# Second-layer groups of fifteen products in two blocks of two steps each

## The chip, the cores and the metric

The kernel runs on one core of a Trainium2 chip. The core has a matrix engine (TensorE, "PE" in the profile; "PEld" is its loading of weights), a vector engine (VectorE, "DVE"), a scalar engine that evaluates functions (ScalarE, "ACT"), a general engine (GpSimd, "POOL") and queues of transfers (started by SyncE, "SP"). Matrix products are accumulated in PSUM, a small memory of eight banks, from which only DVE and ACT read. The metric is the time of one execution on the device, in microseconds (us); less is better.

## The reference

The input x has 2048 rows of 512 numbers. After a layer norm, two branches are computed and multiplied. Branch A is attention with 32 heads of width 16, all on one common set of keys and values; branch B is a layer of 1792 units with the Mish function, and a second layer back to 512.

```python
xn = _layernorm(x)
q  = (xn @ wq)            # 32 heads of 16
k, v = xn @ wk, xn @ wv   # one key and one value head for all
p  = softmax(q k^T / 4)   # 32 x 2048 x 2048
s  = (p v) @ wo
h  = xn @ w1 + b1
g  = silu((h * tanh(softplus(h))) @ w2)
out = x + s * g
```

## The kernel before

**The work of attention.** The 2048 rows are cut into four chunks of 512 (`C`), and the 32 heads into eight sets of four; that makes 32 units of attention, and each unit goes over the 16 blocks of 128 keys. One such block of keys is a *step*; there are 512 steps (`NS`). In a step PE makes four score products `e` (64 rows of the array, 512 columns; L886), ACT takes the exponential of each from PSUM into a tile of `pts` (L893), and two steps later PE multiplies the four tiles with the values (`pv`, L971, on 128 rows, in four column strips of 32; the profile counts eight instructions for one step). The softmax needs the maximum over the keys first: for the units ahead, PE makes four products `m` in each step (L915), and DVE takes the maximum of each from PSUM (L919, one `reduce_max` of 128x512). `e` and `m` have three PSUM banks each (`ps_e`, `ps_m`, L124 and L125), the sum of `pv` and the sum `xps` of the other matrix products one bank each. `pts` has 14 tiles (`NPT`).

**The other matrix products.** They come in *groups* that sum into `xps`: the projection of the queries (`q_group`), the first layer (`m1_group`), the second layer (`m2_groups`) and the output projection (`wo_groups`). Numbers are split in a high and a low part, and three products replace one: a group over four blocks of rows is 12 products. The second layer is cut in thirds of 5, 5 and 4 blocks (`THIRDS`), so that its first two thirds are groups of 15 products and the last is groups of 12; there are 32 groups of 15 (four chunks, two thirds, four tiles of 128 rows). At the end of a group, one engine fetches the sum from `xps`: ACT for the first third (`y<-xps`, L718) and for the first layer (`hb`, L655), DVE for the second and last third (an addition, L722).

**How they share the array.** A product of a group is made in two halves of 64 rows (`half`, L111). In each step one half is used: the halves of the group's products run on 64 rows of the array, while `e` and `m` run on the other 64 rows at the same time. `waves` (L524) writes this interleaving. A group is cut in chunks of at most 8 products (`XMAX`, `chunk_size`); a chunk takes two steps, one for each half. So 12 products are two chunks of 6, and 15 are a chunk of 8 and one of 7; both take four steps. At the end of each step stand ACT's other jobs (`act_jobs`) and the `pv` of two steps before. So the array changes between 64 rows and 128 rows twice in each step.

**What sets the order.** The order of all engines is written by this program itself. The loop at L1312 goes through the steps; `begin` (L472) takes the next group whose operands are thought to be there. What is "there" is found from a count of POOL's time (`busy`, `charge`, `pool_at`) and of SP's (`sp_at`), which are turned into steps with one length for all steps (`STEP_US`, 2.95 us). Weights come by DMA (`load`), and POOL splits them in two parts (`split`); the ring `ws` holds two of the first layer's blocks, the ring `wb` five of the second layer's. Instructions of one engine run in the order in which they are written, so a product whose operand is late holds up all of PE behind it. An instruction that would overwrite a PSUM bank waits for the reader of the bank's last content; a new tile of a pool takes the buffer whose last reader stands earliest in the program.

**Ahead of and behind the steps.** Before step 0 a lead of about 90 us (`LEAD` in the code counts steps at the end) makes the layer norm, the keys and values and the first maxima; PE fills its idle time there with products of groups (`fill`), or with products that nothing uses (`warm`). In the last 22 steps no maxima are left to make, and the rest of the groups runs on all 128 rows between `e` and `pv`.

```python
n = m_sides(1 - h, k // 2) if inm else 0        # m beside the k halves; 4 - n on the halves' own rows
...
waves(h, em, inm)
act_jobs(1 + (len(jobs) > 2))
due(s + 0.5)
if s >= 2:
    pv(s - 2)
```

Of the kernel before, what the change touches and what calls it, by code (L numbers as in the profile page):

```python
# [14 lines left out]
F32 = mybir.dt.float32  # L15
# [5 lines left out]
P = 128  # L21
# [29 lines left out]
TMAX = 2.0 ** 14  # L51
EMAX = 2.0 ** 60
# [33 lines left out]
class Group:  # L86
    def __init__(self, mms, post, items=(), after=(), pre=None, start=None, wo=None, alloc=None):
        self.mms, self.post, self.items, self.after, self.pre = mms, post, items, after, pre
        self.start, self.wo, self.alloc = start, wo, alloc
        self.done = None  # L90
        self.m1 = None
        self.dve = False
        self.late = len(self.items)
        for i in items:
            i.users += 1

    def slack(self, k):
        return 2 if k >= self.late else 0


class Mm:
# [18 lines left out]
def block_kernel(ctx: ExitStack, tc: tile.TileContext, x, wq, wk, wv, wo, w1, b1, w2, out):  # L120
# [13 lines left out]
    lead = {}  # L134
    busy = [-10.0 ** 7]

    def charge(us):
        busy[0] = max(busy[0], step[0] * STEP_US + (0 if lead else 1.5)) + us

    sp_t = [-10.0 ** 7]  # L140

    def sp_at(us):

        sp_t[0] = max(sp_t[0], step[0] * STEP_US) + us
        return (sp_t[0] + 2.6) / STEP_US - 1

    def pool_at(margin):
        return max(math.ceil(2 * (busy[0] / STEP_US + margin)) / 2, step[0])

    def hi_pool(o, i):  # L150
        charge(0.7)
# [231 lines left out]

    def arrived(tag):
        k, n = todo[tag]
        return k < n and items[tag][k].step + 1 <= (step[0] if lead else max(step[0], busy[0] / STEP_US) + 0.3)

    def home(tag, k):
        if tag == "wx":
# [5 lines left out]
    def split(tag):  # L395
        k = todo[tag][0]
        it = items[tag][k]
        w = home(tag, k)
        if not lead:
            busy[0] = max(busy[0], (it.step + 1) * STEP_US)  # L400
# [29 lines left out]
    def load(tag):  # L430
        its = items[tag]
        k, n = todo[tag]
        if tag == "wx" and m1_done.get((NC - 2, NFT - 1)) is None:
            return
        if n == len(its) or n >= RING[tag] and its[n - RING[tag]].users or lead and tag == "wb" and n and now[0] < kept_at.get(3, 1e9):
            return
# [20 lines left out]
            load(tag)  # L457

    held = [None]
    evacs = [0]  # L460
    cur = {"g": None, "ps": None, "n": 0, "chunk": [], "relay": None}

# [8 lines left out]

    def begin():  # L472
        prepare()
        if qqueue and is_ready(qqueue[0]):
# [49 lines left out]
    def waves(h, em, new):  # L524
# [10 lines left out]
        k = len(mms)  # L535
        ms = em(k)
        a = deque(ms[1 - h])
        b = deque(ms[h])
# [38 lines left out]
    def mm12(lhs, rhs, n):  # L577
        res = []
        tot = 3 * n
        for j in range(n):  # L580
            for a, b in TERMS:
                res.append(Mm(pe, lambda j=j, a=a: lhs(j, a), lambda j=j, b=b: rhs(j, b), len(res), tot))
        return res

    qt_of = {}
    xt_done = {}
# [118 lines left out]
    def m2_groups(c, third, its, m1s):  # L705
        lo, hi = THIRDS[third]

        def ready():
            done = m1_done.get((c, hi - 1))
            return None if done is None else done - 2  # L710

        def mk(tt):
            def post(ps):
# [24 lines left out]
                def s3():  # L738
# [5 lines left out]
                later(0.5, lambda: job(s1, t_free))  # L744

            g = Group(mm12(lambda j, a: act_of[c, lo + j][:, a, P * tt:P * (tt + 1)],
                           lambda j, b: its[j].tile[:, b], hi - lo), post, its, [ready])
            g.dve = third > 0
            g.late = 3 if hi - lo == 5 else 2
            return g  # L750
        return [mk(tt) for tt in range(4)]

# [122 lines left out]
    def e_one(s, i):  # L875

        v, r = divmod(s, 16)
        if s < NS - LEAD:
            a, k, p = 1 - s % 2, r - r % 2 + i // 2, i % 2
        else:  # L880
            a, k, p = i % 2, r, i // 2
        q = qt_of[v]
        o = 64 * a
        ps, tag = (ps_m, "m") if NS - LEAD <= s and i in ((1, 3) if s < NS - 8 else (3,)) else (ps_e, "e")
        e = ps.tile([P, C], F32, tag=tag, name=f"e{s}_{i}")
        pe.matmul(e, ks[o:o + 64, P * k:P * (k + 1)], q[o:o + 64, p], start=True, stop=True)  # L886
        z = None
        if i > 1 and s % 4 == 1 and PAIRS[0] < s < PAIRS[1]:
            pt = sb.tile([P, C], F32, tag=("qh", "ql")[i - 2], name=f"pt{s}_{i}", bufs=1)
        else:  # L890
            z = pt_free.popleft()
            pt = pts[:, z]
        r = act.activation(pt, e, AF.Exp, scale=0.25)  # L893
        if z in pt_last:
            tc.declare_no_dep(r.ins, pt_last[z].ins, reason="the value products that read the tile lie between")
        if z is not None:
            pt_last[z] = r
        pt_of[16 * v + k, p, a] = pt, z
        return r

    m_next = [0, 0]

    def m_one(a):
# [5 lines left out]
        kb, j = divmod(n, 8)  # L909
        p, t = divmod(j, 4)  # L910
        o = 64 * a
        ps, tag = (ps_e, "e") if lead and 15 in xp_of and a else (ps_m, "m")
        m = ps.tile([P, C], F32, tag=tag, name=f"m{v}_{a}_{n}")
        o = slice(o, o + (HALF if v < len(qts) else 48))
        pe.matmul(m, q[o, p, P * t:P * (t + 1)], ks[o, C * kb:C * (kb + 1)], start=True, stop=True)  # L915
# [310 lines left out]
    while True:  # L1226
# [46 lines left out]
                task("SP", 2.6, move, [r1])  # L1273
        elif k == "X":
            fresh = cur["g"] is None
            if cur["g"] is not None or not waiting and begun[0] < 1 + (s - 18) / X_US and begin():
# [6 lines left out]
                T["PE"] = s + 0.25  # L1283
                kind[0] = "X"
        elif k == "J":
            tag = next((g for g in ("wq", "ws", "wb") if arrived(g) and busy[0] + E0 < s + 0.5), None)
            n = ran[0]
            if tag:
                split(tag)
# [19 lines left out]
    lead.clear()  # L1309

    rowq = deque()
    for s in range(NS + 2000):  # L1312
        inm = s < NS - LEAD
        if inm or cur["chunk"]:
            assert s < NS
            due(s)
# [53 lines left out]
            if s >= NS:  # L1370
                fill(16)
        step[0] = s
        if vdone[0] < 8 * NC and min(m_next) >= m_need(vdone[0]):
            r = c_rows(vdone[0])
            rowq.extend([r[0], r[1], lambda r=r: (r[2](), r[3]())])
            vdone[0] += 1
        if rowq and not evacs[0]:
            rowq.popleft()()
        evacs[0] = 0
        pump()  # L1380
        if s > NS + 1 and not queue and cur["g"] is None and not timed and not jobs:
            break
# [12 lines left out]
```

## Time and profile before

| | |
|---|---|
| median of 3 runs | 1600.07 us (1599.21 to 1601.7) |
| the profiled execution | 1599.22 us |
| its span, first to last instruction | 1597.4 us |
| PE busy | 1579.5 us, 99% of the span |
| DVE busy | 1345.5 us, 84% |
| ACT busy | 1292.7 us, 81% |
| POOL busy | 620.1 us, 39% |
| mean granted clock of TensorE | 0.999 |

The span is one execution as the hardware profiler saw it; the time has 1.8 us around it. The page shows the busy time of each engine, the span in 40 slices, the chain of work that ended last, and groups of instructions with their mean duration and with the idle time of their engine before them. Two matrix products that run on different rows of the array at the same time both have their own row; so the sum of the durations exceeds the busy time, and what a step costs is read from the starts of the rows. The timeline has one row for instructions of the same kind that follow each other, with their count.

### The profile page before, as it was taken

To read this page: it belongs to the slowest core of one execution; us is meant where nothing else is said; L and a number is where in the kernel's file an instruction comes from. 1 tells how busy PE (TensorE), PEld (TensorE's weight loads), DVE (VectorE), ACT (ScalarE), POOL (GpSimd) and SP (SyncE) were. 2 spreads that over 40 slices of the span, in tenths; PEclk is the share of its full clock that TensorE was granted. 3 is DMA by queue.
4 is the path that set the end of the run, shared out by engine and by line. 5 is a ranking of instruction groups with operands and counts; after the bars stand their busy time and mean duration, and the time that the engine had idled before them with its cause. 6 is when DMAs were issued, how large, how long until landed. Compare 5 with 4: busy or idle time off the path is not lost.

```text
span 1597.4 us, 31240 instructions
## 1 busy us (share of the span) xinstructions
PE 1579.5 (99%) x11660; PEld 843.1 (53%) x11660; DVE 1345.5 (84%) x2299; ACT 1292.7 (81%) x2490; POOL 620.1 (39%) x628
## 2 busy tenths in 40 slices
PE   8999999999999999999999999999999999999998
PEld 5455555555555555555555555555555555555543
DVE  8988888888988988888898988888889998888811
ACT  5478788789898778978889787887898878789785
POOL 3876158155365102422525222252252414226311
PEclk9999999999999999999999999999999999999999
DMA  5332133142141315112113221230332212031020
GB/s 163 146 116 84 35 109 121 27 150 77 45 135 53 103 27 176 57 35 86 50 56 96 76 92 45 96 97 16 123 97 84 73 57 96 16 107 45 17 78 27
DMA packets 72775, 127.30 MB, mean 80 GB/s; under 512 B 21488, under 2 KB 34288, under 8 KB 72112
## 3 DMA queue, kind: packets, MB, share of 16 engines
q1 hardware_dynamic: 72624, 125.30, 25.0%
q8 instruction: 93, 1.52, 0.4%
q14 instruction: 58, 0.48, 0.1%
HBM read 76.36 MB, written 27.26 MB: 65 GB/s over the span
## 4 chain that ended last, share of the span: by engine, by line
PE 93%; DVE 2%; POOL 2%; ACT 2%; DMA 1%; issue 0%; SPq 0%; DVEq 0%; POOLq 0%; ACTq 0%
PE xps L113 46%; PE pv L971 31%; PE m L915 8%; PE e L886 5%; PE xps L109 2%; PE wop L109 1%; DVE mb L919 1%; PE warm L1204 1%; PE kp L296 0%; ACT pts L893 0%; DMA w<-wbs 0%; ACT pts L199 0%; POOL hb L157 0%; DVE st L221 0%; DMA pts<-in_dram 0%
## 5 line engine op out<-in xcount | busy, mean ns | idle before, releaser
L919 DVE TENSOR_REDUCE mb<-m 128x1 f32<-128x512 f32 x2048 | 1271.9, 682 | 177.6 <-PE m L915 151.9
L893 ACT ACTIVATE pts<-e 128x512 f32<-128x512 f32 x2042 | 1065.5, 605 | 245.7 <-PE e L886 237.2
L915 PE MATMUL m<-ks,qt 48*128 48x512 f32 (+1 forms) x2048 | 841.3, 421 | 0.6 <-DVE mb L919 0.2
L886 PE MATMUL e<-qt,ks 64*128 64x512 f32 x2048 | 735.7, 402 | 1.4 <-ACT pt L893 1.4
L971 PE MATMUL pv<-pts,vaug 128*32 128x512 f32 x4084 | 543.8, 604 | 0.0
L915 PEld LDWEIGHTS m<-ks,qt 48*128 48x128 f32 (+1 forms) x2048 | 371.7, 185 | 54.0 <-DVE mb L919 21.2
L886 PEld LDWEIGHTS e<-qt,ks 64*128 64x128 f32 x2048 | 372.9, 186 | 23.0 <-ACT pts L893 12.1
L113 PE MATMUL xps<-xt,ws 64*128 64x512 f32 x1248 | 346.1, 410 | 2.2 <-POOL ws L157 1.2
L113 PE MATMUL xps<-wbs,act 64*128 64x512 f32 x1248 | 337.4, 407 | 0.0
L113 PEld LDWEIGHTS xps<-xt,ws 64*128 64x128 f32 x1248 | 215.1, 185 | 207.4 <-ACT pts L893 135.8
L113 PEld LDWEIGHTS xps<-wbs,act 64*128 64x128 f32 x1248 | 217.5, 185 | 179.4 <-ACT pts L893 112.5
L971 PEld LDWEIGHTS pv<-pts,vaug 128*32 128x32 f32 x4084 | 81.3, 108 | 143.7 <-issue 134.7
L167 POOL TENSOR_SCALAR t<-t 128x512 f32<-128x512 f32 x56 | 34.4, 615 | 310.7 <-ACT t L661 310.4
L157 POOL TENSOR_TENSOR hb<-hb,t 128x512 f32<-128x512 f32 x56 | 72.3, 1290 | 75.7 <-ACT t L674 54.1
L113 PE MATMUL xps<-xt,wq 64*128 64x512 f32 x336 | 93.0, 409 | 0.0
L113 PEld LDWEIGHTS xps<-xt,wq 64*128 64x128 f32 x336 | 58.0, 185 | 55.4 <-ACT pts L893 35.2
L157 POOL TENSOR_TENSOR oc<-oc,sc 128x512 f32<-128x512 f32 (+1 forms) x16 | 20.6, 1285 | 160.7 <-ACT sc L999 121.3
L113 PE MATMUL xps<-wbs,ot_all 64*128 64x512 f32 x288 | 79.3, 408 | 0.0
L113 PEld LDWEIGHTS xps<-wbs,ot_all 64*128 64x128 f32 x288 | 49.5, 184 | 47.0 <-ACT pts L893 29.3
L157 POOL TENSOR_TENSOR hb<-hb,u 128x512 f32<-128x512 f32 x56 | 72.3, 1291 | 4.4
L157 POOL TENSOR_TENSOR act<-hb,act 128x512 fp32r<-128x512 f32 x56 | 72.1, 1287 | 4.7
L157 POOL TENSOR_TENSOR u<-u,t 128x512 f32<-128x512 f32 x56 | 71.9, 1284 | 4.7
(120 smaller groups left out, 814.6 us busy)
## 6 DMA issues: line engine op xcount, KB each, us to landing
ws<-w SPq DMA_DIRECT2D x38, 512.0 KB
wbs<-w SPq DMA_DIRECT2D x36, 512.0 KB
qt<-qh SPq DMA_DIRECT2D x256, 32.0 KB
w<-ws SPq DMA_DIRECT2D x14, 512.0 KB
w<-wbs SPq DMA_DIRECT2D x14, 512.0 KB
wq<-wq SPq DMA_DIRECT2D x13, 512.0 KB
wbs<-wo SPq DMA_DIRECT2D x12, 512.0 KB
rawwb<-in_dram SPq DMA_DIRECT2D x20, 256.0 KB
```

Source lines behind the costliest of these rows:

```text
L109: self.pe.matmul(ps, self.lhs(), self.rhs(), start=(self.k == 0), stop=(self.k == self.tot - 1))
L113: i = self.pe.matmul(ps, self.lhs()[o], self.rhs()[o], start=(self.k == 0 and self.halves == 0), stop=(self.k == self.tot - 1 and self.hal ...
L157: eng.tensor_tensor(out=o, in0=a, in1=b, op=op)
L167: pool.tensor_scalar(o, o, lim, 0.0, op0=ALU.min, op1=ALU.max)
L886: pe.matmul(e, ks[o:o + 64, P * k:P * (k + 1)], q[o:o + 64, p], start=True, stop=True)
L893: r = act.activation(pt, e, AF.Exp, scale=0.25)
L915: pe.matmul(m, q[o, p, P * t:P * (t + 1)], ks[o, C * kb:C * (kb + 1)], start=True, stop=True)
L919: return dve.reduce_max(out=mb_of[v][:, kb, z:z + 1], in_=m, axis=AX.X)
L971: pe.matmul(o[32 * j:32 * j + 32], vaug[:, k], pt, start=(k == 0), stop=(k == 15))
L1204: pe.matmul(w, qts[2][:, 0, 0:P], qts[2][:, 0], start=True, stop=True)
```

## The change

Groups with more than 12 products (so the 32 groups of 15 products of the second layer) no longer go through `waves`. They go through the new `unit`, which fills four steps with two *blocks* of two steps each. In block `h`, all 15 halves of the rows `h` stand in one run, beside eight `e` and seven `m` of the other rows, and one more `m` on the rows `h` at the start; behind them stand two or three jobs of ACT and then the `pv` of two steps, one behind the other. The string `UNIT` is the order in a block. The last `m` of a block takes a bank of `ps_e`. The exponentials of the last two `e` of a block are written behind ACT's jobs (`late`), since only the first of the two `pv` gives the tiles of `pts` back into which they write.

Groups begin only at steps that are multiples of four. The count of time now has its own length for a step without products (2.7 us), with 6 (2.86 us), with 7 or 8 (3.07 us), and for four steps of a `unit` (11.75 us); what lies ahead is counted with 2.88 us for a step. Five instead of three groups of the first layer are put ahead of the second layer (`AHEAD`). At the end of the lead, products of groups may take the place of `warm` products as soon as the first unit's maxima are done. For a `unit`, the operands that are used last may be half a step late by the count, and not two steps.

```diff
-STEP_US = 2.95
+STEP_US = 2.88
+K_US = {0: 2.7, 6: 2.86, 7: 3.07, 8: 3.07}
+UNIT_US = 11.75
+UNIT = "0MEMExEMEMEMEMEm"
-AHEAD = 3
+AHEAD = 5
...
-        if not cur["chunk"] and (not new or cur["g"] is None and not begin()):
+        if not cur["chunk"] and (not new or cur["g"] is None and (step[0] % 4 or not begin())):
             mms = []
...
+    def unit(s, h):
+        g, t = cur["g"], s + 2 * h
+        xs = deque(g.mms)
+        v, r = divmod(s, 16)
+        es = deque((1 - h, r + j // 2, j % 2) for j in range(8))
+        late = []
+        relay = None
+        def x_one():
+            i = xs.popleft().half(cur["ps"], h)
...
+            if h and g.dve and len(xs) == HOLD:
+                held[0] = []
+            if not xs and h:
+                cur["n"] = len(g.mms)
+                finish()
+                for top in held[0] or ():
+                    top()
+                held[0] = None
+        due(t)
+        for n, op in enumerate(UNIT):
+            if n == 8:
+                due(t + 0.5)
+                pump()
+                due(t + 1)
+            if op == "0":
+                m_one(h)
+                op = "E"
+            elif xs:
+                x_one()
+            if op == "E":
+                e = es.popleft()
+                if len(es) > 1:
+                    score(v, *e)()
+                else:
+                    late.append(score(v, *e))
+            elif op in "Mm":
+                relay = m_one(1 - h, op == "m")
+        assert not xs and not es
+        cur["relay"] = relay
+        act_jobs(2 + (len(jobs) > 2))
+        due(t + 1.5)
+        for n in range(2):
+            pv(t + n - 2)
+            if n == 0:
+                for fn in late:
+                    fn()
...
+    for s in range(NS + 2000):
+        inm = s < NS - LEAD
+        if s < skip[0]:
+            continue
+        if s % 4 == 0 and s + 4 <= NS - LEAD and unit_ready(s):
+            for h in range(2):
+                unit(s, h)
+                top_rows(2)
+                evacs[0] = 0
+                pump()
+            base[:] = s + 4, us_of(s) + UNIT_US
+            skip[0] = s + 4
+            continue
```

Of the 490 steps ahead of the last 22, the kernel before fills 360 with 6 products, 64 with 8, 63 with 7 (one more stands just behind), and leaves three without. The changed kernel fills 358 with 6, 128 in 32 units, two with 3 (the rest of a group that the lead began) and leaves two without.

On PE, at the second layer's second third in the second chunk of rows (`xps` the sum, `act` its operand, `m`, `e` and `pv` as above): before, one `pv` of one step between two runs of products.

```order
L113 MATMUL xps<-wbs,act_9_8717 128x512
L886 MATMUL e_3_9202<-qt_77,ks 128x512
L915 MATMUL m_1_30_9205<-ks,qt_78 128x512
L971 MATMUL pv_8921<-pts,vaug 32x512 x4
L113 MATMUL xps<-wbs,act_7_6938 128x512
L915 MATMUL m_1_31_9214<-ks,qt_78 128x512
L113 MATMUL xps<-wbs,act_8_8471 128x512
L886 MATMUL e_0_9218<-qt_77,ks 128x512
```

Now, at the same group, the end of its first block and the start of its second.

```order
L117 MATMUL xps<-wbs,act_9_8079 128x512
L966 MATMUL e_3_1_1_9527<-qt_77,ks 128x512
L117 MATMUL xps<-wbs,act_9_8079 128x512
L994 MATMUL m_1_18_9530<-ks,qt_79 128x512
L1050 MATMUL pv_8930<-pts,vaug 32x512 x8
L994 MATMUL m_1_19_9560<-ks,qt_79 128x512
L966 MATMUL e_0_0_0_9563<-qt_78,ks 128x512
L117 MATMUL xps<-wbs,act_5_6461 128x512
```

Two `pv` stand together (x8 for x4), and all 15 products (blocks 5 to 9 of `act`) have passed before them; the next run begins with block 5 again, on the other rows.

On DVE, at the end of the same group (`mb` the maxima, `y` the second layer's sum): before, the addition stands between the reductions of steps that have four each.

```order
L919 TENSOR_REDUCE mb_9193<-m_1_0_9222 128x1
L919 TENSOR_REDUCE mb_9193<-m_1_1_9230 128x1
L722 TENSOR_TENSOR y_0_7639<-xps,y_0_7639 128x512
L919 TENSOR_REDUCE mb_9193<-m_0_1_9242 128x1
L919 TENSOR_REDUCE mb_9193<-m_0_2_9257 128x1
```

Now it stands behind seven of a block's eight reductions, and ahead of the eighth, whose `m` lies in a bank of `ps_e`.

```order
L998 TENSOR_REDUCE mb_9221<-m_0_9_9434 128x1
L998 TENSOR_REDUCE mb_9221<-m_0_10_9441 128x1
L795 TENSOR_TENSOR y_0_7846<-xps,y_0_7846 128x512
L998 TENSOR_REDUCE mb_9221<-m_0_11_9449 128x1
L998 TENSOR_REDUCE mb_9221<-m_0_12_9469 128x1
```

The bank of that eighth `m` is the one which the first `e` of the next block takes, so this `e` now stands behind an addition and a reduction of DVE.

On POOL, about the twelfth block of weights of the first layer (`ws11`; numbers are shown, the first after a name counts the blocks; `hb`, `t` and `u` are the Mish function's tiles, `wbs` the second layer's weights): before, it is split behind two blocks of the second layer's second third.

```order
L152 TENSOR_SCALAR ws10_2759<-rawws10_2708 128x512
L157 TENSOR_TENSOR ws10_2759<-rawws10_2708,ws10_2759 128x512
L152 TENSOR_SCALAR wbs_101<-rawwb8_2712 128x512
L157 TENSOR_TENSOR wbs_101<-rawwb8_2712,wbs_101 128x512
L152 TENSOR_SCALAR wbs_101<-rawwb9_2764 128x512
L157 TENSOR_TENSOR wbs_101<-rawwb9_2764,wbs_101 128x512
L152 TENSOR_SCALAR ws11_2924<-rawws11_2886 128x512
L157 TENSOR_TENSOR ws11_2924<-rawws11_2886,ws11_2924 128x512
```

Now it is split before the second layer's first group begins, right behind the tenth first-layer block's first Mish instructions.

```order
L180 TENSOR_SCALAR t0_9_2024<-t0_9_2024 128x512
L735 TENSOR_SCALAR u0_9_2025<-t0_9_2024 128x512
L170 TENSOR_TENSOR u0_9_2025<-u0_9_2025,t0_9_2024 128x512
L170 TENSOR_TENSOR hb0_9_1974<-hb0_9_1974,u0_9_2025 128x512
L165 TENSOR_SCALAR ws11_2035<-rawws11_1989 128x512
L170 TENSOR_TENSOR ws11_2035<-rawws11_1989,ws11_2035 128x512
```

The split of `ws11` moved ahead of the blocks `wb5` to `wb9`, by about a whole third of the second layer.

More of the change, by code (lines that the diff above doesn't have):

```diff
@@ L97, in slack @@
     def slack(self, k):
-        return 2 if k >= self.late else 0
+        return self.most if k >= self.late else 0
 class Mm:
@@ L385, in arrived @@
         k, n = todo[tag]
-        return k < n and items[tag][k].step + 1 <= (step[0] if lead else max(step[0], busy[0] / STEP_US) + 0.3)
+        return k < n and items[tag][k].step + 1 <= (step[0] if lead else max(step[0], step_of(busy[0])) + 0.3)
     def home(tag, k):
@@ L473, in begin @@
         prepare()
-        if qqueue and is_ready(qqueue[0]):
+        last_wo = queue and queue[0].wo is not None and wo_left[queue[0].wo] == 1 and is_ready(queue[0])
+        if qqueue and is_ready(qqueue[0]) and not (last_wo and step[0] < qqueue[0].after[0]() + 5):
             g = qqueue.popleft()
@@ L911, in m_one @@
         o = 64 * a
-        ps, tag = (ps_e, "e") if lead and 15 in xp_of and a else (ps_m, "m")
+        ps, tag = (ps_e, "e") if other or lead and 15 in xp_of and a else (ps_m, "m")
         m = ps.tile([P, C], F32, tag=tag, name=f"m{v}_{a}_{n}")
@@ L1285, in block_kernel @@
         elif k == "J":
-            tag = next((g for g in ("wq", "ws", "wb") if arrived(g) and busy[0] + E0 < s + 0.5), None)
+            tag = next((g for g in ("wq", "ws", "wb") if arrived(g) and busy[0] + E0 < s + (4.5 if g == "ws" else 0.5)), None)
             n = ran[0]
@@ L1372, in block_kernel @@
         step[0] = s
[L1373 to L1378, printed above, removed]
+        top_rows(0 if evacs[0] else 1)
         evacs[0] = 0
+        base[:] = s + 1, us_of(s) + K_US.get(halves[0], STEP_US)
         pump()
```

89 lines of the change are left out of this document (63 added, 26 removed).

## The prediction

> **What bounds the kernel now.** I read the page first (busy times, the chain that ended last, the groups), then a table by stretches, then the timeline of PE around groups of fifteen.
>
> ```profile
> span 1597.4 us, 31240 instructions
> ...
> PE 1579.5 (99%) x11660; PEld 843.1 (53%) x11660; DVE 1345.5 (84%) x2299; ACT 1292.7 (81%) x2490; POOL 620.1 (39%) x628
> ...
> POOL 3876158155365102422525222252252414226311
> ...
> PE 93%; DVE 2%; POOL 2%; ACT 2%; DMA 1%; issue 0%; SPq 0%; DVEq 0%; POOLq 0%; ACTq 0%
> ...
> L919 DVE TENSOR_REDUCE mb<-m 128x1 f32<-128x512 f32 x2048 | 1271.9, 682 | 177.6 <-PE m L915 151.9
> L893 ACT ACTIVATE pts<-e 128x512 f32<-128x512 f32 x2042 | 1065.5, 605 | 245.7 <-PE e L886 237.2
> ```
>
> The chain that ended last is PE for 93%. DVE and ACT wait for PE (151.9 and 237.2 us), not the reverse: both have room on the average. Whether that holds in the middle is seen in a stretch without the lead and the end:
>
> ```profile
> 490.00:890.00 400.00, 400.00 (x3072) 214.98 (x3070) 352.39 (x599) 332.55 (x641) 138.22 (x137) 1.00 0.24 73
> ```
>
> PE has no idle time there, the granted clock is 1.00, DVE is busy for 352 of 400 us and ACT for 333. So time can be won only in how PE's instructions follow each other, and DVE has 12% left.
>
> The timeline of PE, one step of 6 products and then four groups of 15 (only the rows used):
>
> ```profile
> 666.92 1.06 PE L971 MATMUL pv<-pts,vaug 128*32 128x512 f32 x8
> ...
> 669.43 0.41 PE L886 MATMUL e<-qt,ks 64*128 64x512 f32 x1
> 669.76 1.06 PE L971 MATMUL pv<-pts,vaug 128*32 128x512 f32 x8
> 670.76 0.50 PE L113 MATMUL xps<-wbs,act 64*128 64x512 f32 x1
> 670.76 0.50 PE L915 MATMUL m<-ks,qt 48*128 48x512 f32 x1
> 671.10 0.39 PE L113 MATMUL xps<-wbs,act 64*128 64x512 f32 x1
> ...
> 672.49 0.39 PE L113 MATMUL xps<-wbs,act 64*128 64x512 f32 x1
> ...
> 718.99 1.07 PE L971 MATMUL pv<-pts,vaug 128*32 128x512 f32 x8
> ```
>
> A step of 6 takes 669.76 - 666.92 = 2.84 us. From 669.76 to 718.99 lie 16 steps, four groups of 15: 12.31 us for a group. Inside a step: from `pv` to the first pair 1.00; first to second pair 0.34; then (672.49 - 671.10) / 6 = 0.232 for each pair; from the last pair to `pv` 0.33. So either side of `pv` costs about 0.1 more than a pair does. What two `pv` in a row cost is seen near the end:
>
> ```profile
> 1529.98 1.92 PE L971 MATMUL pv<-pts,vaug 128*32 128x512 f32 x16
> 1531.83 0.96 PE L886 MATMUL e<-qt,ks 64*128 64x512 f32 x6
> ```
>
> Two steps' `pv` take 1.85 up to the next product; the second adds 0.85.
>
> **The units, if nothing waits.** A block is 16 pairs and two `pv`: 1.85 + 0.34 + 14 x 0.232 + 0.33 = 5.77 us, a unit 11.54. Against 12.31 that is 0.77 less, and for 32 units 24.6 us. The pairs are as many as before (four times 8); what goes is two changes between 64 and 128 rows for each group. This is the upper end. The Trainium skill, "TensorE: Matmul & The Clock Gate", Part 2, "Back-to-back issue gap", gives about 216 ns for 512 columns at full clock; with it each block would be 0.23 us shorter, and the sum 14.5 us lower. The 0.232 of the rows is measured on these very pairs and decides.
>
> **What DVE takes back.** In a block, `m` stands at pairs 0, 1, 3, 7, 9, 11, 13 and 15, and there are three banks; the last goes into a bank of `ps_e`.
>
> ```profile
> 75.54 7.25 DVE L919 TENSOR_REDUCE mb<-m 128x1 f32<-128x512 f32 x12
> ...
> 671.33 2.48 DVE L919 TENSOR_REDUCE mb<-m 128x1 f32<-128x512 f32 x4 [0.37 <-PE m L915]
> ```
>
> A reduction starts 0.57 after its `m` (671.33 - 670.76), and in a row they follow every (7.25 - 0.68) / 11 = 0.597 us. Counted from a block's first pair, the fourth reduction runs from 2.36 to 3.04; the seventh `m`, at 0.34 + 12 x 0.232 = 3.12, needs its bank: with 0.08 us for the release (below) it is free just in time. The eighth reduction ends at 0.57 + 7 x 0.597 + 0.68 = 5.43, ahead of the next block at 5.77, whose first `e` takes that bank. So without an addition nothing waits. In the 16 units of the second third, DVE's addition (512 numbers on 128 rows from PSUM, counted like a reduction) stands ahead of the eighth reduction, which then ends at 6.03; with the release the first `e` starts at 6.11 and not at 5.77: 0.34 us, and behind this `e` all of PE. After 10 of the 16 another unit follows; after the others a step, whose first `e` comes one pair later, at 0.34. I take 10 x 0.34 = 3.4 us; bounds 0 and 64 x 0.34 = 21.8 (every block).
>
> **What ACT takes back.** A unit has 16 exponentials and the other jobs: (1292.7 - 1065.5) / 512 = 0.44 us for a step, 1.8 for four. With (1.60 - 0.605) / 2 = 0.5 us from one exponential to the next (the row below) that is 9.8 of 11.5, but jobs come in lumps. What a lump costs shows in a step of 6:
>
> ```profile
> 484.53 0.76 ACT L670 ACTIVATE t<-u,two 128x512 f32<-128x512 f32 x1
> 485.14 1.60 ACT L893 ACTIVATE pts<-e 128x512 f32<-128x512 f32 x3
> ```
>
> ```profile
> 485.62 0.39 PE L915 MATMUL m<-ks,qt 48*128 48x512 f32 x1
> 485.82 0.50 PE L886 MATMUL e<-qt,ks 64*128 64x512 f32 x1
> ```
>
> The `e` that belongs beside the `m` of 485.62 waits until the first exponential of the row at 485.14 has left its bank (485.14 + 0.6 = 485.74, and 0.08 for the release): 0.2 us. In a unit the jobs stand behind six exponentials, ahead of the two late ones, which wait for the first `pv` in any case: two or three jobs from 3.4 to 5.0, `pv` done at 3.92 + 1.07 = 4.99. So inside a run of units ACT's jobs are covered; the cover ends if a job waits for POOL. A unit behind a plain step (13 of 32 in the order) meets the step's job at its first exponentials: 13 x 0.2 = 2.6. To that 0.07 for each unit, as the four groups above have over four undisturbed steps of 8 pairs (1.00 + 0.34 + 6 x 0.232 + 0.33 = 3.06; 12.31 - 12.24): 2.2. Together 4.8; bounds 0 and 0.2 for each of 64 blocks, 12.8.
>
> Units: 24.6 - 3.4 - 4.8 = 16.4 us won; 11.80 us for a unit.
>
> **The weights.** Two steps of the kernel before wait for POOL's split of first-layer weights:
>
> ```profile
> 235.03 0.40 PE L886 MATMUL e<-qt,ks 64*128 64x512 f32 x1
> 236.04 0.50 PE L113 MATMUL xps<-xt,ws 64*128 64x512 f32 x1 [0.62 <-POOL ws L157]
> ...
> 246.06 1.07 PE L971 MATMUL pv<-pts,vaug 128*32 128x512 f32 x8
> 247.98 0.50 PE L113 MATMUL xps<-xt,ws 64*128 64x512 f32 x1 [0.85 <-POOL ws L152]
> ...
> 249.33 0.49 PE L113 MATMUL xps<-xt,ws 64*128 64x512 f32 x1 [0.62 <-POOL ws L157]
> ...
> 250.69 0.64 PE L971 MATMUL pv<-pts,vaug 128*32 128x512 f32 x4
> ```
>
> The first costs about 0.9 us (236.04 - 235.03 against 0.23, and a little at its start), the second 4.63 - 2.84 = 1.8. The first is for `ws11`, which now is split some 20 steps ahead of its group; I take that 0.9 as won. The second, for `ws12`, has the same distance as before (its load can start only when the group two before it ends), and stays. Bounds: both go (-2.7), or the run of five first-layer groups that now stands at the start (steps 4 to 23) has three such waits of its own (+5.4).
>
> **The end, and what costs nothing.** The last 22 steps have one stretch of 8 products on 128 rows less, since two steps with 6 now stand ahead of them:
>
> ```profile
> 1532.72 2.13 PE L109 MATMUL xps<-xt,act 128*128 128x512 f32 x8
> ...
> 1554.82 3.60 PE L109 MATMUL xps<-xt,act 128*128 128x512 f32 x8
> ```
>
> ```profile
> 1550.00:1559.00 9.00, 7.81 (x38) 3.75 (x40) 0.51 (x1) 7.81 (x17) 5.00 (x5) 0.81 0.23 85
> ```
>
> Four products less in a stretch are 4 x 0.27 = 1.1 us; I take 1.0. The second stretch ran at a lower clock (0.81 over 9 us, in which PE was idle for 1.2): 1.5 us that may go, or come at another place. Bounds -2.5 and +2. The Trainium skill, "TensorE: Matmul & The Clock Gate", Part 1, says that the clock halves after a window without work; the row agrees, 0.45 us for a product against 0.27. In the lead, nine products take the place of `warm` products on an idle PE; DVE's maxima end the lead, so I count 0 (bounds 0 and +0.5, if the product's weights come late). Groups at every fourth step leave no more empty steps than before (two, and two with 3, for three): 0. The rows of maxima for the next unit of attention come at the earliest two steps before their use, as before.
>
> Sum: -16.4 - 0.9 - 1.0 = -18.3 us. The profiled execution took 1599.22, so 1580.9; it lies 0.85 below the median of 1600.07, from which the same sum gives 1581.8. I say 1582.
>
> **Rivals.** *Nothing waits in the units:* 24.6 + 1.9 = 26.5 less, 1573.6, and down to 1569 with the bounds of weights and end. For it: no reduction is late by the sum, but the seventh `m` has no room. Against: ACT's lumps.
>
> *Fetching from PSUM takes over.* If DVE starts 0.34 late in each block, its seventh `m` waits that long, and if each block's first `e` waits as after an addition, it is as much: 24.6 - 21.8 + 1.9 = 4.7 less, 1595. For it: eight `m` in 3.9 us, where DVE needs 4.8 for eight; before it was four in 3.06. Against: the `pv` stretch of 1.85 lets it catch up, and 16 x 0.597 + 0.6 = 10.2 is below 11.5. By the Trainium skill, "TensorEngine Tiling (Array Packing)", "PSUM Bottleneck", fetching from PSUM may become the bound once tiles speed up PE; here DVE's 88% in the middle agrees that it is near.
>
> *Slower: first-layer weights late.* The order now asks for five first-layer groups in a row at the start, with 11.4 us between them, while POOL also splits the second layer's first blocks. Each block that is late as at 246.06 costs 1.8. It decides against the change from 18.3 + 3.2 = 21.5 us on: twelve late blocks, 1603 and more. For it: POOL has the digits 8 and 7 in ten in the page's second and third slices. Against: 0.39 busy over all, and no wait but two before.
>
> **Numbers.** Forecast (1576 to 1587) 0.56; nothing waits (below 1576) 0.12; PSUM (1587 to 1597) 0.18; no change 0.04; slower 0.10. A measurement here tells 0.2%, 3.2 us, from nothing. So faster 0.86, same 0.04, slower 0.10. The range from 1573 to 1594 leaves out slower, same, and the outer part of two rivals, some 0.18.
>
> **What would show it.** Sixteen instructions of `pv` in a row, 32 x 2 times, 1.85 us up to the next pair; units of 11.6 to 11.9 us from `pv` to `pv`; waits of `e` for DVE of 0.3 after additions only; the wait at `ws11` gone. Wrong if units take over 12, if `m` waits for DVE in most blocks, or if PE waits for POOL in the first 200 us.

## The result, and the profile after

The changed kernel takes 1586.58 us (median of four runs, 1585.45 to 1589.18), the kernel before 1600.16 beside it (1599.21 to 1601.70). The ratio is 0.9917, with an interval from 0.9899 to 0.9934: 13.6 us faster, where 18.3 were forecast.

The page of the changed kernel, the lines that answer to those of before:

```profile
span 1585.5 us, 31218 instructions
...
PE 1567.0 (99%) x11649; PEld 876.2 (55%) x11649; DVE 1342.0 (85%) x2299; ACT 1296.2 (82%) x2492; POOL 622.6 (39%) x630
...
POOL 3787527617446221450542323054044232405212
...
PE 93%; ACT 2%; DVE 2%; POOL 1%; DMA 1%; issue 0%; SPq 0%; DVEq 0%; POOLq 0%; ACTq 0%
...
L998 DVE TENSOR_REDUCE mb<-m 128x1 f32<-128x512 f32 x2048 | 1266.0, 681 | 171.5 <-PE m L994 112.1
L971 ACT ACTIVATE pts<-e 128x512 f32<-128x512 f32 x2042 | 1062.2, 606 | 217.7 <-PE e L966 152.4
...
L994 PEld LDWEIGHTS m<-ks,qt 48*128 48x128 f32 (+1 forms) x2048 | 368.0, 185 | 115.6 <-DVE mb L998 67.3
```

PE is still the chain. What has grown is the last row: the loading of the keys' weights for `m` stands idle for 115.6 us, 67.3 of it by the profile because of DVE. On the page of before it was half of that:

```profile
L915 PEld LDWEIGHTS m<-ks,qt 48*128 48x128 f32 (+1 forms) x2048 | 371.7, 185 | 54.0 <-DVE mb L919 21.2
```

Below it turns out that this row names the wrong engine.

The timeline of PE and ACT in the changed kernel, one block of a unit from value products to value products:

```profile
689.49 1.92 PE L1050 MATMUL pv<-pts,vaug 128*32 128x512 f32 x16
...
691.34 0.50 PE L994 MATMUL m<-ks,qt 48*128 48x512 f32 x1
...
691.68 0.39 PE L117 MATMUL xps<-wbs,act 64*128 64x512 f32 x1
...
691.91 3.05 ACT L971 ACTIVATE pts<-e 128x512 f32<-128x512 f32 x6 [0.26 <-PE e L966]
...
694.48 0.62 PE L117 MATMUL xps<-wbs,act 64*128 64x512 f32 x2
...
695.01 0.50 PE L994 MATMUL m<-ks,qt 48*128 48x512 f32 x1
...
695.44 1.92 PE L1050 MATMUL pv<-pts,vaug 128*32 128x512 f32 x16
```

Sixteen `pv` stand in a row, and from them to the first pair it is 691.34 - 689.49 = 1.85 us, to the second 0.34, as in the forecast. But the block takes 695.44 - 689.49 = 5.95 us and not 5.77. Its last `m` starts at 695.01, 0.05 after the sixth exponential (691.91 + 3.05 = 694.96), into the bank that this one frees; the products of the group run ahead of it, and the next `pv` waits for it.

Where the time went is counted from two executions whose clock fell neither in the lead nor at the end, the profiles of the runs "a0" (the changed kernel) and "p0" (the kernel before) below, with spans of 1583.8 and 1595.6 us:

| part | before | changed | difference | forecast |
|---|---|---|---|---|
| lead, up to the first `pv` | 96.4 | 96.0 | -0.4 | 0 |
| 32 groups of 15 | 392.7 (12.27 each) | 382.4 (11.95 each) | -10.3 | -16.4 |
| waits at steps 50 and 54 | 2.4 | 0 | -2.4 | -0.9 |
| stall at steps 58 and 59 | 0 | 5.6 | +5.6 | 0 |
| other steps | | | -1.5 | 0 |
| last 22 steps and what follows | 76.31 | 73.65 | -2.7 | -1.0 |
| sum | 1595.6 | 1583.8 | -11.7 | -18.3 |

The medians lie further apart (13.6 us): the execution counted for the kernel before took 1597.43 us, 3 us less than the median of its run, at a granted clock of 1.000; that of the changed kernel took 1585.63, close to its run's median.

Ahead of the last 22 steps lie 127 of the 128 steps of the groups of 15 in the kernel before; they take 389.7 us, and 392.7 is that scaled to 128. The 382.4 are 64 blocks with 371.9 us, and the 10.5 that the twelve steps behind a run of units are longer than other steps of 6, because their span holds the unit's second `pv`.

The stall is new. In the profile of the changed kernel it looks like this, SP, POOL, ACT and PE in turn, each from the timeline of its engine:

```profile
233.56 7.26 SPq L461 DMA_DIRECT2D rawwb<-in_dram  x2
...
252.26 0.40 SPq L459 DMA_DIRECT2D rawws<-in_dram  x1
```

```profile
256.06 0.62 POOL L165 TENSOR_SCALAR ws<-rawws 128x512 fp32r<-128x512 f32 x1 [6.82 <-DMA rawws<-in_dram]
...
259.97 0.62 POOL L180 TENSOR_SCALAR t<-t 128x512 f32<-128x512 f32 x1
...
261.38 1.26 POOL L170 TENSOR_TENSOR u<-u,t 128x512 f32<-128x512 f32 x1
```

```profile
262.67 0.72 ACT L741 ACTIVATE t<-u,two 128x512 f32<-128x512 f32 x1 [3.17 <-POOL u L170]
```

```profile
258.52 1.06 PE L1050 MATMUL pv<-pts,vaug 128*32 128x512 f32 x8
263.93 0.50 PE L966 MATMUL e<-qt,ks 64*128 64x512 f32 x1 [2.52 <-ACT pts L971]
264.36 1.06 PE L1050 MATMUL pv<-pts,vaug 128*32 128x512 f32 x8
```

SP is held for 7.26 us at two raw loads (of weights that POOL has not split yet) and so issues the raw weight `rawws` late; by the code there are two raw buffers (`RAWS`), and the split that frees one ends on POOL at 240.5 us, as SP goes on. POOL waits 6.82 us for it, with the Mish instructions of another group queued behind the split; ACT's logarithm waits for those, with exponentials queued behind it; PE's `e` waits 2.52 us for a bank. The late weight stops no product of its own.

### The profile page after: what moved, and what is told of

The parts are those of the page before. It is cut to its first block, busy times and chain, and to the rows that moved or that the text cites. A ratio compares the mean times of both kernels' runs of the same rounds, so it can differ in the third digit from the quotient of the medians.

```text
span 1585.5 us, 31218 instructions
## 1 busy us (share of the span) xinstructions
PE 1567.0 (99%) x11649; PEld 876.2 (55%) x11649; DVE 1342.0 (85%) x2299; ACT 1296.2 (82%) x2492; POOL 622.6 (39%) x630
## 4 chain that ended last, share of the span: by engine, by line
PE 93%; ACT 2%; DVE 2%; POOL 1%; DMA 1%; issue 0%; SPq 0%; DVEq 0%; POOLq 0%; ACTq 0%
PE xps L117 42%; PE pv L1050 31%; PE m L994 12%; PE e L966 6%; PE xps L113 2%; ACT pts L971 1%; DVE mb L998 1%; PE kp L309 1%; PE wop L113 1%; ACT pts L212 0%; PE warm L1283 0%; DMA pts<-in_dram 0%; DVE st L234 0%; DMA rawws<-in_dram 0%; PE xp L270 0%
## 5 line engine op out<-in xcount | busy, mean ns | idle before, releaser
L966 PE MATMUL e<-qt,ks 64*128 64x512 f32 x2048 | 746.4, 408 | 4.3 <-ACT pts L971 3.6
L1050 PE MATMUL pv<-pts,vaug 128*32 128x512 f32 x4084 | 530.8, 603 | 0.0
L994 PEld LDWEIGHTS m<-ks,qt 48*128 48x128 f32 (+1 forms) x2048 | 368.0, 185 | 115.6 <-DVE mb L998 67.3
L966 PEld LDWEIGHTS e<-qt,ks 64*128 64x128 f32 x2048 | 371.9, 186 | 28.9 <-ACT pts L971 16.9
L117 PE MATMUL xps<-xt,ws 64*128 64x512 f32 x1230 | 341.4, 410 | 0.2 <-POOL ws L170 0.2
L117 PE MATMUL xps<-wbs,act 64*128 64x512 f32 x1248 | 313.5, 396 | 0.0
L117 PEld LDWEIGHTS xps<-wbs,act 64*128 64x128 f32 x1248 | 226.8, 185 | 63.5 <-ACT pts L971 29.3
L1050 PEld LDWEIGHTS pv<-pts,vaug 128*32 128x32 f32 x4084 | 88.1, 108 | 151.7 <-issue 143.7
```

The source lines that it names most:

```text
L117: i = self.pe.matmul(ps, self.lhs()[o], self.rhs()[o], start=(self.k == 0 and self.halves == 0), stop=(self.k == self.tot - 1 and self.hal ...
L1050: pe.matmul(o[32 * j:32 * j + 32], vaug[:, k], pt, start=(k == 0), stop=(k == 15))
```

## The experiments

**The changed kernel again (run "a0"), and the kernel before again ("p0").** No edit.

> The changed kernel once more. In its profiled execution the granted clock fell to 0.51 and 0.63 between 40 and 48 us, and the lead came out 2.5 us longer than before, in instructions that stand in the same order in both kernels. Theory: this fall of the clock isn't part of the change; it is in some executions and not in others, so here the first product with the values may start as early as in the kernel before (96.3 + 0.4 us) and the time be 1585 to 1589. Rival: the lead of the changed kernel always has it; then the window from 40 to 48 us shows a clock under 0.7 again.

Measured: 1585.74 us (1584.68 to 1586.48), ratio 0.9909 (0.9893 to 0.9924). A row of a stretch gives its start and end, its length, the busy time (with the number of instructions) of PE, PEld, DVE, ACT and POOL, the granted clock, and the share and the GB/s of the transfers. The first two rows are the changed kernel's first profile, the other two that of this run:

```profile
39.00:48.00 9.00, 9.00 (x28) 3.83 (x26) 6.59 (x12) 7.24 (x14) 5.09 (x4) 0.62 0.31 106
264.00:270.00 6.00, 6.00 (x33) 2.94 (x35) 2.88 (x5) 4.62 (x9) 5.67 (x7) 0.72 0.01 2
```

```profile
39.00:48.00 9.00, 9.00 (x34) 3.66 (x33) 8.51 (x15) 6.98 (x14) 6.12 (x5) 1.00 0.44 160
261.00:267.00 6.00, 5.80 (x23) 2.63 (x23) 2.03 (x3) 3.59 (x8) 5.67 (x7) 0.50 0.13 52
```

The clock that PE was granted fell to 0.62 in the lead of the one execution and not in the other, with the same instructions; the first `pv` starts at 98.83 and at 95.98 us. So the lead isn't longer by the change. At steps 58 and 59 the clock fell in both, behind the wait of 2.5 us: half of what is lost there is the wait, half the clock.

> The kernel before once more, for a second profile of it. In the first one the end (from the last value product ahead of the last 22 steps on) took 77.8 us, with a stretch at a clock of 0.66 to 0.75 from 1554 to 1560 us; in the changed kernel 73.7. The run with the old lead, which has as many products of the second layer there as the kernel before, took 75.4. Theory: 1.75 us of the difference is the order, 2.4 the stretch and its idle time, and those belong to that one execution; then the end takes 75 to 76 here. Rival (the wait and the fall behind it come from the order of the kernel before): 77 to 78 again.

Measured: 1600.55 us (1596.73 to 1602.20), ratio 0.9996. The same place at the end, first in the profile of before, then in this one:

```profile
1554.00:1560.00 6.00, 6.00 (x24) 3.21 (x28) 0.00 (x0) 4.81 (x10) 4.46 (x5) 0.72 0.00 0
```

```profile
1554.00:1560.00 6.00, 6.00 (x34) 2.91 (x34) 0.00 (x0) 5.01 (x12) 4.21 (x5) 1.00 0.00 0
```

PE's wait of 1.19 us ahead of it stands in both; the fall of the clock stands in one. In this run the wait is this row:

```profile
1553.65 0.98 PE L886 MATMUL e<-qt,ks 64*128 64x512 f32 x2 [1.19 <-ACT pt L893]
```

The end takes 76.3 us here and 77.8 there. The theory said 75 to 76 and the rival 77 to 78: the clock (1.5 us) belongs to that execution, as the theory had it, but the idle time stays, so the order's part is 76.31 - 73.65 = 2.7 us and not 1.75.

**The units alone undone ("e4").**

```diff
-        return ok and 12 < len(cur["g"].mms) <= len(UNIT) - 1
+        return False
```

> The units alone undone: groups of 15 go in chunks of 8 and 7 over four steps as before; lead, order of groups, beginnings at every fourth step and the count of time stay. Theory (the second run of value products is what wins): four steps take 12.28 us in place of 11.95, 32 x 0.33 = 10.5 us more than the changed kernel, so 1597. Rival (the gain comes from the other parts, and a block's waits eat what the units win): within 3 us of the changed kernel, 1584 to 1590.

Measured: 1592.77 us (1592.39 to 1595.46), ratio 0.9957 (0.9940 to 0.9973). Neither number: 6 to 7 us above the changed kernel. The 128 steps of the groups of 15 take 392.3 us here, 12.26 for a group, so the units themselves are worth 392.3 - 382.4 = 9.9, near the 10.5 of the theory. The rest is the stall, which differs: PE's wait there is 1.59 us, with no fall of the clock, and the two steps take 2.1 us too long in place of 5.6. The other parts of the change are then worth 1600.8 - 1592.8 = 8.0 us by the medians, and 4.6 by the spans of the two executions with a profile (1595.6 in "p0", 1591.0 here); which of the two is nearer isn't shown.

**What paces a block ("e1", "e2", "e3").** Three edits in the units: the exponentials on half of their columns, the maxima on half, both. The lines that hand the width `w` on are left out here, and so is the factor of all exponentials, which is 0.02 in place of 0.25 where the maxima are halved.

```diff
-            x = act.activation(dst, e, AF.Exp, scale=0.25)
+            x = act.activation(dst[:, :w], e[:, :w], AF.Exp, scale=0.25)
```

```diff
-            return dve.reduce_max(out=mb_of[v][:, kb, z:z + 1], in_=m, axis=AX.X)
+            return dve.reduce_max(out=mb_of[v][:, kb, z:z + 1], in_=m[:, :w], axis=AX.X)
```

> In the units each exponential takes only 256 of its 512 columns (the other half of the scores is left out there). A second or later block takes 5.95 us from value product to value product, where 5.77 was worked out. Theory A: its last product m waits for the sixth exponential of the block, so ACT paces the block; then blocks of 5.77 to 5.82, 64 x 0.15 = 9.6 us less, about 1576. Rival B (DVE paces it, by the bank that the fourth reduction frees for the seventh m): 5.95 as now, 1586. Rival C (PE needs 5.95 of its own): 5.95 too.

> In the units each maximum takes only 256 of its 512 columns (half of the keys is left out of the maxima there; the exponentials have a smaller factor, so that they stay finite, at the same cost). Theory A (ACT paces the block): 5.92 to 5.95, the time within 2 us of the changed kernel. Rival B (DVE paces it): 5.77 to 5.82, and the blocks that follow DVE's addition, now 6.02, as well; about 1576. Rival C: 5.95.

> In the units exponentials and maxima both take 256 of 512 columns. What is left is what PE needs for a block when no bank is late. By the sum of the prediction 5.77 for a later block and 4.92 for the first after a plain step: 11 to 12 us less than the changed kernel, 1574. Rival C (the waits are not the cause, PE needs 5.95): no change. If the halved ACT alone or DVE alone gives nothing and both together give 5.77, both end at the same time and A and B are both true.

Measured: 1577.04 us (two executions, 1575.72 to 1578.37), 1586.05 (three, 1585.02 to 1588.19) and 1573.12 (two, 1572.17 to 1574.08). The `pv` of two neighbouring blocks from each timeline of PE, half exponentials, half maxima, both:

```profile
686.18 1.92 PE L1050 MATMUL pv<-pts,vaug 128*32 128x512 f32 x16
...
692.01 1.92 PE L1050 MATMUL pv<-pts,vaug 128*32 128x512 f32 x16
```

```profile
687.67 1.92 PE L1050 MATMUL pv<-pts,vaug 128*32 128x512 f32 x16
...
693.62 1.92 PE L1050 MATMUL pv<-pts,vaug 128*32 128x512 f32 x16
```

```profile
683.73 1.92 PE L1050 MATMUL pv<-pts,vaug 128*32 128x512 f32 x16
...
689.51 1.92 PE L1050 MATMUL pv<-pts,vaug 128*32 128x512 f32 x16
```

5.83, 5.95 and 5.78 us. Theory A holds: ACT paces the block. With ACT out of the way DVE holds it at 5.83, 0.12 us below what ACT allows and 0.05 above what is left with both halved. Over all units, counted as above: 382.4 us as changed, 381.9 with half maxima, 373.4 with half exponentials, 370.1 with both. So ACT's part is 9.0, DVE's 0.5 alone and 3.3 once ACT is out of the way, and with both halved a unit takes 11.57 us. Rival C falls. The row of the page on idle weight loads, with half exponentials and with half maxima:

```profile
L994 PEld LDWEIGHTS m<-ks,qt 48*128 48x128 f32 (+1 forms) x2048 | 368.9, 186 | 108.7 <-DVE mb L998 66.0
```

```profile
L994 PEld LDWEIGHTS m<-ks,qt 48*128 48x128 f32 (+1 forms) x2048 | 368.8, 186 | 114.4 <-issue 40.1
```

Where 9 us were won, the row still puts 66.0 us down to DVE; where DVE no longer leads it, nothing was won. The loads run ahead of the products, and their idle time isn't PE's.

**SP's count of time ("e5", again in "e5b", and beside that the changed kernel once more, "a0b").** The plan is told that a raw load waits for the buffer of the load two before it.

```diff
+            if not lead and len(loaded) >= RAWS:
+                sp_t[0] = max(sp_t[0], getattr(loaded[-RAWS], 'free', 0) or busy[0] + 2)
+            loaded.append(it)
             it.raw, it.step = r, (lead["arrive"]() if lead else sp_at(0.45))
```

Here `free` is POOL's count of time at the end of the split that reads the buffer.

> Only the count of SP's time is changed: the load of a raw weight also counts the time until the split before it has freed the buffer. PE's order stays word for word; POOL, ACT and SP change places in a few spots, so that POOL's split of a late weight stands behind the Mish work and not ahead of it. Theory (the 4.4 us lost at steps 58 and 59 come from POOL waiting 6.8 us for a raw weight with Mish work queued behind it, and ACT waiting for that with exponentials queued behind): both waits go, 4.4 us less than the changed kernel, 1582. Rival (the weight's landing itself is the limit): the wait moves to the products of that weight, 0 to 1 us won, 1586.

> The kernel of e5 once more, beside the changed kernel on the same chip, for the size of its gain. Theory: 5.3 us fewer in the steps, as its profile shows, 1580 to 1584 by how often the lead's clock falls, the changed kernel 1584 to 1589.

> The changed kernel beside the two others on the same chip. Theory: 1584 to 1589; the clock falls at 261 to 267 us, behind the wait at steps 58 and 59, in every profiled execution. Rival: the fall there is by chance, as in the lead.

Measured: 1583.51 (1580.68 to 1583.78) and 1581.48 us (1580.92 to 1582.76), ratios 0.9891 both times (0.9874 to 0.9908); the changed kernel beside the first ("a0") 1585.74, beside the second 1586.26 (1583.43 to 1588.70), ratio 0.9916 (0.9902 to 0.9931). So the median is 2.2 us lower the first time and 4.8 the second. POOL in this kernel at the place of the stall:

```profile
248.72 0.61 POOL L180 TENSOR_SCALAR t<-t 128x512 f32<-128x512 f32 x1
...
254.02 0.62 POOL L165 TENSOR_SCALAR ws<-rawws 128x512 fp32r<-128x512 f32 x1 [1.24 <-DMA rawws<-in_dram]
```

SP is held as long as before (7.14 us), but the Mish work now stands ahead of the split and fills POOL's idle time. PE's wait is gone, and with it the fall of the clock: the steps take 1408.9 us, 5.3 less than in "a0". The theory holds; by the profile there is more to win than its 4.4. In the third profile of the changed kernel ("a0b") the clock fell behind the stall too, to 0.57 from 264 to 267 us, and this time also at 96 to 99 us, to 0.50. The rival, chance, isn't excluded by that: in "e3", behind a wait of 2.90 us at the same steps, the clock did not fall.

**The order of groups ("e6", "e7").** First the lead's three conditions as before (one of the three is shown), then three groups ahead in place of five.

```diff
-            if cur["g"] is not None or not waiting and (vdone[0] or begun[0] < 1 + (s - 18) / X_US) and begin():
+            if cur["g"] is not None or not waiting and begun[0] < 1 + (s - 18) / X_US and begin():
```

```diff
-AHEAD = 5
+AHEAD = 3
```

> The lead alone as before: no group is begun in place of the products that keep PE busy at the lead's end, and the three conditions on loads and jobs in the lead are the old ones. The order of groups moves by four steps. Theory (the 2.5 us that the lead took longer are the clock and not the new products): the first product with the values starts within 0.5 us of where it starts in the changed kernel in an execution without the fall of the clock, and the total is the same within 3 us, 1584 to 1590, up or down by where weights come late. Rival (the products in the lead cost it): 2.5 us earlier, 1583 to 1585.

> Three first-layer groups in place of five ahead of the first second-layer group (AHEAD 3, as before the change); all else as in the changed kernel. Theory: the lead over the weights of 11 and 12 that the two more groups give took away the two waits at steps 50 and 54 (2.7 us), and the stall at 58 and 59 (4.4 to 5.8 us) belongs to the new order; so here the two waits come back and the stall goes: 1 to 3 us less than the changed kernel, 1583 to 1585. Rival (the stall belongs to the count of time, not to the order): a stall of some 4 us stays at some step before 110 beside the two waits, 1588 or more.

Measured: 1588.43 us (1586.77 to 1589.45), ratio 0.9922 (0.9903 to 0.9942), and 1589.20 (1585.59 to 1591.56), ratio 0.9927 (0.9899 to 0.9956). The old lead: its rival falls, it isn't faster; but its profile shows two falls of the clock ahead of the first `pv` (0.50 at 42 to 45 us and at 81 to 84), so that the first `pv` came at 101.8 us, and the size of the lead's part can't be read from it. Its steps have no stall (1410.4 us), and its end takes 75.4 us, with 55 products of the second layer in it and not 42.

With three groups ahead the theory falls: the two waits at 50 and 54 don't come back, and the stall stays and only moves. At step 90 POOL waits in the same way:

```profile
349.13 0.62 POOL L165 TENSOR_SCALAR ws<-rawws 128x512 fp32r<-128x512 f32 x1 [7.25 <-DMA rawws<-in_dram]
```

So the stall doesn't come from the two more groups ahead; it comes from the count of time, as "e5" shows. The order still decides where it stands, and with the old lead, which moves the order by four steps, it doesn't stand anywhere. What took away the two waits at 50 and 54 isn't shown: it wasn't the two more groups. The order also changes the end: 77.8 us here, with 70 products of the second layer.

**The lead's idle time filled ("b1")**, on top of the kernel of "e5".

```diff
     def v_transpose(c):
+        if c and cur["g"] is None and not waiting:
+            w = ps_x.tile([P, C], F32, tag="x", name="warmx")
+            for _ in range(2):
+                pe.matmul(w, qts[2][:, 0, 0:P], qts[2][:, 0], start=True, stop=True)
```

> The kernel of e5 and, in the lead, two products without use ahead of each transposition of values from the second chunk of keys on, into the bank of xps, where PE now waits 0.75 us for DVE (at 37.8 us) and 0.6 (at 50.3). Theory: the fall of the clock from 39 to 47 us, 2.5 us in the profiled executions that have it, follows this idle time; then no execution has it, and the median is that of e5 in an execution without it, 1580 to 1582. Rival (the fall comes from elsewhere, such as the moment at which the execution starts): it stays in about half of the executions, the median within 1 us of e5's.

Measured: 1580.65 us, four executions from 1580.57 to 1580.78; ratio 0.9883 (0.9870 to 0.9897), faster than the kernel before and the changed one, and 0.8 us under "e5b" beside it. PE in the lead, from 36 to 39 us, first the changed kernel ("a0b"), then this one:

```profile
36.00:39.00 3.00, 2.22 (x18) 1.70 (x16) 2.83 (x5) 2.96 (x8) 0.00 (x0) 1.00 0.22 49
```

```profile
36.00:39.00 3.00, 2.87 (x18) 1.77 (x17) 2.90 (x6) 2.96 (x8) 0.00 (x0) 1.00 0.25 55
```

The theory agrees: the executions of e5's kernel lie up to 3.1 us apart, these four 0.2. With four executions, and a fall that came in 4 of the 13 profiles with the idle time, this speaks for the theory but doesn't settle it.

## Why the prediction was right, and where it was not

- **Faster, within the range, in part by luck.** The time lies 0.4 us under the upper end of 1576 to 1587. By the table the units won 6.1 less than forecast and the stall cost 5.6 that no term held; the lead (0.4), the waits (1.5), the other steps (1.5) and the end (1.7) gave more than forecast and brought 5.1 of these 11.7 back.
- **The main reason holds.** The units win by having fewer places where a `pv` stands between runs of products; undoing them alone costs 9.9 us. Whether it is the change between 64 and 128 rows that costs time there, or something else about a `pv`, no run separates. What PE needs was worked out as 5.77 for a block and 11.54 for a unit and measures 5.78 and 11.57 with ACT and DVE halved. So without waits the units would have won 392.7 - 370.1 = 22.6, against 24.6 in the forecast; the waits took 382.4 - 370.1 = 12.3, against 3.4 + 4.8 = 8.2.
- **"So without an addition nothing waits"** is the step that failed. It followed DVE's three banks and said of the last `m` only that it goes into a bank of `ps_e`; when that bank comes free was not asked. The eight `e` and this `m` are nine products in three banks, so the `m` needs the sixth exponential to end. That is at 0.57 + 5 x 0.49 + 0.6 = 3.62, counted from the first pair; with 0.05 for the release the `m` starts at 3.67, and not at 0.34 + 14 x 0.232 = 3.59. Having waited, it lasts 0.50 and not 0.39, and the `pv` comes 0.43 after it and not 0.33. That is some 0.17 in each of 64 blocks. The forecast's own 0.5 and 0.6 give 0.57 + 2.5 + 0.6 = 3.67 for the end of the sixth exponential, but its text on ACT let the jobs behind it start at 3.4.
- **DVE's addition, 3.4 us**, measures 0.6 at most (the half maxima won 0.5 in all). Seven blocks behind an addition take 6.02 to 6.04 in "a0", some 0.08 more than the others and not 0.34.
- **ACT's lumps, 4.8 us**: ACT was the right engine and the wrong mechanism. Its jobs are covered, as the text said, but for eight blocks of 6.08, each the first behind the end of a unit of attention, where ACT fetches the sum of `pv` (0.61 us) ahead of the six exponentials: some 1.1 us in all. The rest of ACT's 9.0 us is the row of six exponentials itself.
- **PSUM as the bound**, the second rival, came true by half: the fetch takes over in every block, by ACT and by 0.17 us, where it was priced by DVE and at 0.34. The Trainium skill, "TensorEngine Tiling (Array Packing)", "PSUM Bottleneck", says that after a faster TensorE the fetching may become the bound, and tells to use both engines for it; the traces agree with the first, and here both were in use and reach their limits within 0.12 us of each other (5.95 and 5.83).
- **The weights, -0.9.** Both waits went (2.4 us, near the lower bound of 2.7), the second too, which was to stay; the "three such waits" of the upper bound didn't come at steps 4 to 23 (0.7 us there in all, 0.23 of it PE's idle time for POOL, one of the signs of being wrong, in small). A stall in their place came through ACT's queue, which the third rival had not: it looked for late weights at the products that use them.
- **The end, -1.0**: 2.7, just over the bound. Four products fewer were counted; there are six fewer on 128 rows (42 and not 48), and the seven halves of step 490 are gone too. PE's busy time there falls by 2.4 us. PE's waits hardly change: that of 1.19 us went with the order, but in place of 1.40 us in all there are three of 0.32 to 0.45, together 1.12. The stretch at a lower clock was rightly said to be able to go or to come elsewhere.
- **The lead, 0**: holds, -0.4.
- **The signs.** The sixteen `pv` and the 1.85 us are there. A unit takes 11.95 on the average, above the 11.6 to 11.9 that were to show the forecast right and under the 12 that were to show it wrong.

## What to carry to other kernels

Where a block of work is made longer between two fixed points, ask for each bank that its last products take when it comes free, over all engines that give banks back, and not for one engine's banks alone; a row of idle time that names an engine is no proof, halving that engine's work is. A late load needn't hurt where it is used: look at what is queued behind the instruction that waits for it, on each engine in turn. Before a few microseconds of a lead or an end are explained by an edit, look at the granted clock in a second profile of the same kernel.

## What the runs showed of the hardware

The granted clock falls to 0.50 behind short idle times of PE, and not each time. Behind 0.75 to 0.81 us of idle time in the lead it fell in 4 of 13 profiles; behind 1.19 us at the end of the kernel before in one of two; behind 1.63 us at 79 us in "e6", and not behind the 1.59 us of the stall in "e4"; behind the waits of 2.4 to 2.9 us at the stall in six of seven. Each fall lasted 3.41 or 6.83 us; one of the first kind cost 1.5 us (the end of the kernel before), one of the second 2.9 (the lead, 98.83 - 95.98). In five of the 14 profiles it also fell at 96 to 101 us, where PE had no idle time over 0.15 us in the 5 us before; what brings these falls isn't shown, and the products without use in "b1" do not stand there. The Trainium skill, "TensorE: Matmul & The Clock Gate", Part 1, says that the window that is watched is about 3.4 us and runs freely, so that the same kernel can meet it in another phase; that the falls come and go agrees with it, and so do their lengths, one or two such windows. Its rule that idle times of over about 3.4 us bring the fall doesn't cover these falls: all idle times here were shorter, that of 1.19 us too on which the prediction saw its row agree with a window without work, and the measurement decides.

Half the columns cost ACT more than half: two exponentials in a row of 128x256 take 0.66 us, of 128x512 1.08.
